# Retention, MoE layer and 8 capacity-bound experts on one core: where searches, results and stage borders are emitted

## The chip, the cores and the metric

The kernel runs on 1 core of one Trainium2 chip. The metric is the device time of one execution in microseconds, as the median of several runs; before the change it is 1059.77 us (3 runs, 1058.21 to 1059.84).

## The reference

Three layers follow one another. A retention (a linear attention with a decay per head) over 4 batches of 768 positions gives `x` of 3072 tokens by 512 features. A dense layer with 2048 hidden features follows. Then each token goes to one of 8 experts, greedily by the largest gate logit over all pairs of token and expert, with at most 384 tokens for an expert:

```python
    # retention, per step t
    state = gamma * state + einsum('bhd,bhe->bhde', k[t], v[t])
    y[t] = scale * einsum('bhd,bhde->bhe', q[t], state)
    # dense layer
    r = np.maximum(x @ w_in, 0.0)
    x = (s * (r * r) + b) @ w_out
    # experts
    logits = x @ w_gate
    for idx in np.argsort(-logits.flatten()):
        tok, e = (int(idx) // E, int(idx) % E)
        if assigned[tok] >= 0 or counts[e] >= cap:
            continue
        assigned[tok] = e
        counts[e] += 1
    for e in range(E):
        mask = assigned == e
        out[mask] = np.maximum(x[mask] @ w1[e], 0.0) @ w2[e]
```

## The kernel before

**Precision.** Every product is made of three: both operands are split into a high part (`xh`, `rh`, `gh`, `hh`, the weights' `h`) and a low part (`xl`, `rl`, `gl`, `hl`, `l`), and high·high, high·low and low·high are summed. ScalarE (ACT) makes the high part by a copy to the short format, VectorE (DVE) the low part by a subtraction, and TensorE (PE) needs both.

**Stages.** The 3072 tokens are 12 blocks of 256. Blocks 0 to 2 run through the dense layer while the weights are converted (48 to 181 us in the profiled execution), then blocks 3 to 9 (190 to 556 us). The attention of a block is made while the block ahead of it is in the dense layer; between the stages, at 181 to 190 and at 556 to 570 us, the attention of block 3 and of the last two blocks stands alone. An attention chunk is `b_part` (scores, masked by DVE to `am`, L331) and `c_part` (products with `am` and the state `sbd`, then `xh` on ACT and `xl` on DVE, L352 to L373). Blocks 10 and 11 go last: `h_pair` makes their hidden features f = 0 to 15 (for each f 12 products of 256 columns for either block, L422; Relu, Square and Copy on ACT, L425 to L434), `l_unit` their logits (L678), and `x_last` their outputs (L694), which also fill the time in which the first search runs (626 to 701 us). The experts' products follow, 701 to 1041 us: `eh_unit` (L1060, 12 products of 384 columns for each of 8 f), `eh_out` (the low part `hl`, L1069) and `ey_unit` (L1081, the outputs, from the third f on).

**A search** (generator `search`, L829 to L919) finds which expert closes next and the threshold for its tokens. It goes through six digits: `count` on PE (24 small products, L817), then on DVE `b`, `sat`, `jj`, `d`, and the next digit's `cmp` (L809). From the last count's result a chain of small DVE instructions gives `stb` and `ei`, the number of the closed expert, which SyncE reads to fetch that expert's weights `eraw`. Then `ca` (the count, written with `sat`, L891), the total `tot` (L894), `tots` on ACT (L896) and the slot product (L908, L909) follow. `begin` prepares the next search (`Lm` to `Eh` on DVE, `EH` on ACT, L765 to L809), and `index` (L927 to L961) turns slots into row numbers by `ob`, `oa`, `pay` on DVE and a product L947. `fetch` gathers the tokens `xg` by these numbers, transposes them and makes `gh` (ACT, L1001) and `gl` (DVE, L1002). `prep` splits an expert's raw weights: `h` on ACT (L1032), `l` on DVE (L1041).

**What sets the order.** Each engine executes its instructions in the order in which they were emitted. The emission is woven by hand: `Weave.unit(cost, fn)` emits one unit of PE's work and moves a clock of its own, `t`, on by `cost`; before it, each `Side` (a generator) whose due time has been reached takes a step, and what the generator yields is added to its due time. So the numbers in SY, IY, FE and BG, in ns of that clock, are pauses between the pieces of a search (SY), an index (IY), a fetch (FE) and `begin` (BG). They set no time on the chip, only what stands ahead of what.

Of the kernel before, what the change touches and what calls it, by code (L numbers as in the profile page):

```python
# [20 lines left out]
F32 = mybir.dt.float32  # L21
# [60 lines left out]
def kernel(  # L82
# [15 lines left out]
    stages=2,  # L98
    FC=((5, 0), (1, 0), (0, 1), (0, 0), (0, 0), (0, 0)),
    CY=(700, 1200),  # L100
    SY=(2900, 3200, 2700, 0, 1800, 800),
    IY=(600, 4600, 800),
    LG=(900, 880),
    FE=(9000, 3000),
    FZ=(8390, 1300),
    BG=(450,),
    WARM=24,
# [28 lines left out]
    def bank(i):  # L136
        return psum.tile([128, 512], F32, name=f"b{i}", tag=f"b{i}")
# [18 lines left out]
    work = p1.enter_context(tc.tile_pool(name="work", bufs=2))  # L156
    xpool = p1.enter_context(tc.tile_pool(name="xpool", bufs=2))
    tmp = p1.enter_context(tc.tile_pool(name="tmp", bufs=6))

    QKV = {}  # L160
    QD = {}
# [119 lines left out]
    def retention(blk, wide):  # L281

        if blk == NB - 1:

            XF.extend(tmp.tile([128, 512], F32, name="tmp").rearrange("p (a b) -> p a b", b=TB) for _ in range(2))
        elif blk == 2:
            xh = stage.tile([128, NP, TB], F32R, name="xhs", tag="sb")
            xl = stage.tile([128, NP, TB], F32R, name="xls", tag="sb")
        else:
            xh = xpool.tile([128, NP, TB], F32R, name="xh")  # L290
            xl = xpool.tile([128, NP, TB], F32R, name="xl")
        if blk < NB - 1:
            XT[blk] = (xh, xl)
        c0 = 2 * (blk % BPB)
# [19 lines left out]
        def b_part(j):  # L314

            if j == 0 and c0 == 0:
                pST[0] = bank(4)
            if wide:
                scale_next(j)
            qT, kT, kt, vt = views(j)  # L320
            ps = [bank(i) for i in ((6, 7) if not wide or j == 0 else (0, 1))]
# [58 lines left out]

        return scale_gen, b_part, c_part

    def attn(blk, wide):
        scale_gen, b_part, c_part = retention(blk, wide)
        for j in range(2):
            if not wide:
                yield from scale_gen(j)
            yield from b_part(j)
            if wide:
                yield 1500  # L390
                if j:
                    c_part(0)
                    yield 2500
            else:
                yield 4500
                c_part(j)
                yield 9000
        if wide:
            c_part(1)
            yield 2500  # L400
# [1 line left out]
    X2, R2 = {}, {}  # L402

    def split_last():
        xh = xpool.tile([128, NP, TB], F32R, name="xh")
        xl = xpool.tile([128, NP, TB], F32R, name="xl")
        XT[NB - 1] = (xh, xl)
        for i in range(2):
            ps = slice(2 * i, 2 * i + 2)
            ACT.activation(xh[:, ps], XF[i], AF.Copy)  # L410
            DVE.tensor_tensor(xl[:, ps], XF[i], xh[:, ps].bitcast(F32), op=OP.subtract)

    def h_unit(blk, f, hb):

        xh, xl = XT[blk]
        wh, wl = W[2 * f]
        ph = bank(hb)[:, 0:TB]
        n = 0
        for kc in range(KC):
            ks = slice(kc * 128, (kc + 1) * 128)  # L420
            for a, b in ((wh, xh), (wh, xl), (wl, xh)):
                PE.matmul(ph, a[:, ks], b[:, kc, :], start=(n == 0), stop=(n == 3 * KC - 1))  # L422
                n += 1
# [169 lines left out]
        convert(FC[j][1])  # L593
    conv.due = 0.0
    wv = Weave([conv])
    for u in moe1((0, 1, 2), ((4, 5), (6, 7), (0, 1)), 2):
        wv.unit(*u)
    conv_until(NF - 1)
    load_chunk(CPB)
    load_chunk(CPB + 1)  # L600
    scale_chunk(CPB)
    load_gate()
    a4 = Side(attn(3, True), wv.t)
    wv.add(a4)
    wv.until(lambda: a4.done)
    tail = Side(logits_gen())
    wv.add(tail)
    def attn2():
        for b in (NB - 2, NB - 1):
            yield from attn(b, False)  # L610

    for blk in range(3, NB - 2):
        nxt = Side(attn(blk + 1, False) if blk < NB - 3 else attn2(), wv.t + 4000 * (blk == 3))
        wv.add(nxt)
        units = moe1((blk,), ((0, 1),), 2)
        for i, u in enumerate(units):
            if i == len(units) - 2:
                while not nxt.done:
                    nxt.step()
                if blk == NB - 3:  # L620
                    split_last()
            wv.unit(*u)
    p0.close()
# [35 lines left out]
    for t in stbs:  # L659
        POOL.memset(t, 0.0)  # L660

    pair = (NB - 2, NB - 1)
    R4 = {}
    ERAW = {}

    def h_pair(f):
        rs = []
        for i, blk in enumerate(pair):
            wv.unit(1320, lambda: rs.append(h_unit(blk, f, 2 + i)))

        R4[f] = W[2 * f]
        for i, r in enumerate(rs):
            r_split(r, *(t[:, i * TB:(i + 1) * TB] for t in R4[f]))
        low_parts()

    def l_unit(f):
# [152 lines left out]
    def search(i):  # L829
# [11 lines left out]
        else:  # L841
# [3 lines left out]
            for s, w in enumerate(BW):  # L845
# [9 lines left out]
                    DVE.scalar_tensor_tensor(b, d, up, digit(key, s + 1), op0=OP.mult, op1=OP.add)  # L855
                else:
                    DVE.tensor_scalar(b, d, 1.0, None, op0=OP.add)

                sat = rt.tile([128, NT], BF, name="sat")
                sa = rt.tile([128, 1], F32, name="sa")  # L860
# [22 lines left out]
        ei = rt.tile([1, 1], I32, name="ei", bufs=3)  # L883
        DVE.tensor_scalar(ei, sm[0:1, :], -1.0, float(E), op0=OP.mult, op1=OP.add)
        EV[i] = ei
        yield SY[4]

        if not last:

            ca = rt.tile([128, 1], F32, name="ca")  # L890
            DVE.scalar_tensor_tensor(sat[:, 0:NL], iota[:, 0:NL], jj, cnt[:, 0:NL], op0=OP.is_equal, op1=OP.mult,  # L891
                                     accum_out=ca)
        tot = bank(6)
        PE.matmul(tot[:, 0:128], stb, ones_b, start=True, stop=True)  # L894
        tots = rt.tile([128, 128], BF, name="tots")
# [68 lines left out]
    def fetch(i):  # L964
# [10 lines left out]
        gh = ff.tile([128, KC, CAP], F32R, name="gh")  # L975
        gl = ff.tile([128, KC, CAP], F32R, name="gl")

        def turn(pt, t, kc):
            PE.transpose(pt[:, t * 128:(t + 1) * 128], xg[:, t, kc * 128:(kc + 1) * 128], ident)

# [13 lines left out]
        for kc in range(KC):  # L994
# [4 lines left out]
            else:  # L999
                pt = pts[kc]  # L1000
            ACT.activation(gh[:, kc, :], pt[:, 0:CAP], AF.Identity, bias=cT[:, kc:kc + 1])  # L1001
            DVE.scalar_tensor_tensor(gl[:, kc, :], pt[:, 0:CAP], cT[:, kc:kc + 1], gh[:, kc, :].bitcast(F32),  # L1002
                                     op0=OP.add, op1=OP.subtract)
            if i and kc < 3:
                prep(i, kc)
            if i and kc < KC - 1:
                yield FE[1]
        XG[i] = (gh, gl)
        HOLD.clear()

# [82 lines left out]
    def mlp(i):  # L1093
        units = []

        for f in range(NF2 + 1):
# [3 lines left out]
            for t in range(GT):  # L1100
# [2 lines left out]
                    if g >= 0:  # L1103
                        units.append((650, lambda g=g, t=t: ey_unit(i, g, t)))
                if f < NF2 and t == 0:
                    units.append((0, lambda f=f: (eh_out(i, f), prep(i, f + 3))))
                if f == NF2:
                    units.append((0, lambda t=t: e_out(i, t)))
        return units
# [128 lines left out]
```

## Time and profile before

| | |
|---|---|
| median of 3 runs | 1059.77 us |
| profiled execution, its own time | 1049.21 us |
| its span | 1047.4 us |
| PE busy | 991.0 us (95%) |
| DVE busy | 720.4 us (69%) |
| ACT busy | 459.2 us (44%) |
| GpSimd busy | 76.7 us (7%) |
| granted TensorE clock, mean | 0.99 |
| chain that ended last | PE 73%, DVE 12%, issue 8%, ACT 3%, DMA 2% |

All rows come from one profiled execution. PE's waits are listed by who released them: "PE b L894 <- DVE sat L891" means that the product of line 894 stood still until DVE's instruction of line 891 had ended. A time given for a wait is PE's idle time just before the product. An instruction's second number in a timeline is its duration, which for PE's pipelined products is longer than the distance between two starts; the distance is what counts for PE. In a table by stretches the x in brackets is the number of instructions, and PEclk the granted clock, 1.00 being 2.4 GHz.

### The profile page before, as it was taken

Reading aid. Unit: us, or ns where it says so; the run is one execution under the profiler, and the core shown is the slowest. Engines: PE = TensorE matmul, PEld = TensorE weight load, DVE = VectorE, ACT = ScalarE, POOL = GpSimd, SP = SyncE. Lnnn points to the kernel's source line nnn. Section 1 sums busy time; section 2 is a strip of 40 time slices with the busy share of each in tenths; the row PEclk is TensorE's granted clock in tenths of the full one; section 3 lists DMA queues with packets and bytes.
Section 4 is the critical chain, followed back from the end, with each engine's and each line's share of the span. In section 5 each row is a group of like instructions: output and inputs, shape, how many; then the busy total and the mean of one; then the engine's idle time right before and its main releaser. Section 6 shows DMA issues by size and latency. Waiting matters only on the chain.

```text
span 1047.4 us, 19172 instructions
## 1 busy us (share of the span) xinstructions
PE 991.0 (95%) x7548; PEld 875.5 (84%) x7548; DVE 720.4 (69%) x1794; ACT 459.2 (44%) x935; POOL 76.7 (7%) x100
## 2 busy tenths in 40 slices
PE   6899999999999999999998999889888898999997
PEld 5789988889899999899997987758766787888996
DVE  4799993687887787887744525786797877455521
ACT  1567665444344444344443661431443343434531
POOL 4100002100000000000000000011202020220211
PEclk8999999999999999999999999999999999999999
DMA  8433353431221212121120000531343424344520
GB/s 291 175 119 123 127 172 135 127 123 57 69 71 52 66 57 58 65 71 52 52 72 30 2 1 1 191 122 32 113 130 103 141 82 158 126 159 161 176 96 31
DMA packets 35035, 104.34 MB, mean 100 GB/s; under 512 B 4737, under 2 KB 5377, under 8 KB 34945
## 3 DMA queue, kind: packets, MB, share of 16 engines
q1 hardware_dynamic: 30384, 89.49, 25.9%
q0 software_dynamic: 3840, 12.59, 3.7%
q8 instruction: 59, 0.97, 0.4%
q10 hardware_dynamic: 720, 1.05, 0.3%
q14 instruction: 32, 0.25, 0.1%
HBM read 90.52 MB, written 12.58 MB: 98 GB/s over the span
## 4 chain that ended last, share of the span: by engine, by line
PE 73%; DVE 12%; issue 8%; ACT 3%; DMA 2%; POOL 1%; SPq 0%; POOLq 0%; ACTq 0%; DVEq 0%
PE b L422 24%; PE b L451 19%; PE b L1060 7%; PE b L1081 7%; PE b L694 3%; PE b L352 2%; PE b L325 2%; PE b L817 2%; PE b L362 2%; DVE l L1041 2%; ACT EH L785 1%; PE b L358 1%; DMA qdec0h<-in_dec_dram 1%; DVE raw L263 1%; POOL out_dram L1087 1%
## 5 line engine op out<-in xcount | busy, mean ns | idle before, releaser
L474 DVE SCALAR_TENSOR_TENSOR scr<-tmp,wg 128x512 bf16<-128x512 f32 x288 | 199.3, 692 | 9.0 <-ACT tmp L461 4.1
L422 PE MATMUL b<-xh,l 128*128 128x256 f32 x704 | 199.4, 283 | 3.4 <-DVE l L267 3.4
L422 PE MATMUL b<-xh,h 128*128 128x256 f32 x704 | 199.4, 283 | 1.5 <-ACT xh L372 1.5
L422 PE MATMUL b<-xl,h 128*128 128x256 f32 x704 | 199.3, 283 | 0.3 <-DVE xl L373 0.3
L425 ACT ACTIVATE r<-b 128x256 f32<-128x256 f32 x192 | 73.6, 383 | 212.2 <-PE b L422 203.4
L422 PEld LDWEIGHTS b<-xh,h 128*128 128x128 f32 x704 | 134.4, 191 | 9.6 <-ACT xh L372 1.7
L422 PEld LDWEIGHTS b<-xl,h 128*128 128x128 f32 x704 | 134.5, 191 | 6.1 <-DVE xl L373 0.5
L422 PEld LDWEIGHTS b<-xh,l 128*128 128x128 f32 x704 | 134.6, 191 | 3.8 <-DVE l L267 3.8
L451 PE MATMUL b<-h,rh 128*128 128x512 f32 x320 | 129.3, 404 | 0.0
L451 PE MATMUL b<-h,rl 128*128 128x512 f32 x320 | 125.7, 393 | 2.2 <-DVE rl L441 2.2
L451 PE MATMUL b<-l,rh 128*128 128x512 f32 x320 | 126.5, 395 | 0.0
L441 DVE TENSOR_TENSOR rl<-r,rh 128x256 fp32r<-128x256 f32 x160 | 68.5, 429 | 41.9 <-ACT rh L434 41.8
L1060 PE MATMUL b<-gh,h 128*128 128x384 f32 x256 | 90.7, 354 | 3.5 <-DVE hl L1069 3.2
L1069 DVE SCALAR_TENSOR_TENSOR hl<-b,hh 128x384 fp32r<-128x384 f32 x64 | 35.5, 554 | 79.0 <-ACT hh L1063 79.0
L1060 PE MATMUL b<-gl,h 128*128 128x384 f32 x256 | 86.6, 338 | 0.7 <-DVE gl L1002 0.7
L1060 PE MATMUL b<-gh,l 128*128 128x384 f32 x256 | 86.4, 338 | 0.0
L433 ACT ACTIVATE r<-r 128x256 f32<-128x256 f32 x192 | 79.9, 416 | 5.1
L1063 ACT ACTIVATE hh<-b 128x384 fp32r<-128x384 f32 x64 | 31.3, 489 | 115.8 <-PE b L1060 114.4
L1081 PE MATMUL b<-h,hh 128*128 128x512 f32 x192 | 78.3, 408 | 0.0
L1041 DVE TENSOR_TENSOR l<-eraw,h 128x1024 fp32r<-128x1024 f32 x64 | 77.8, 1216 | 0.7 <-ACT h L1032 0.7
L1081 PE MATMUL b<-h,hl 128*128 128x512 f32 x192 | 75.9, 395 | 0.0
L1081 PE MATMUL b<-l,hh 128*128 128x512 f32 x192 | 75.7, 394 | 0.0
(234 smaller groups left out, 1779.8 us busy)
## 6 DMA issues: line engine op xcount, KB each, us to landing
eraw<-in_w_dram SPq DMA_DIRECT2D x64, 512.0 KB, 4.0
q<-in_qkv_dram SPq DMA_DIRECT2D x36, 512.0 KB, 4.8
raw<-in_w_dram SPq DMA_DIRECT2D x32, 512.0 KB, 4.4
x2d<-tmp SPq DMA_DIRECT2D x20, 256.0 KB, 5.6
qdec<-in_dec_dram SPq DMA_DIRECT2D x18, 256.0 KB, 2.7
wg<-in_wgT_dram SPq DMA_DIRECT2D x4, 512.0 KB, 6.2
x2d<-tmp ACTq DMA_DIRECT2D x3, 256.0 KB, 3.3
first0h<-in_qkv_dram SPq DMA_DIRECT2D x2, 256.0 KB, 4.1
```

The source lines that it names most:

```text
L422: PE.matmul(ph, a[:, ks], b[:, kc, :], start=(n == 0), stop=(n == 3 * KC - 1))
L425: ACT.activation(r, ph, AF.Relu)
L433: ACT.activation(r, r, AF.Square)
L441: DVE.tensor_tensor(rl, r, rh.bitcast(F32), op=OP.subtract)
L451: PE.matmul(X2[blk][t], a[:, ts], b, start=(f == 0 and i == 0), stop=(f == NF - 1 and i == 2))
L474: DVE.scalar_tensor_tensor(scr, x, 1.0, WG[e], op0=OP.mult, op1=OP.mult, accum_out=of[:, e:e + 1])
L694: PE.matmul(XB[c][:, ns], a[:, cs], b[:, ns], start=(f == 0 and i == 0), stop=(f == NF - 1 and i == 2), skip_group_check=True)
L1041: DVE.tensor_tensor(lo, raw, hi.bitcast(F32), op=OP.subtract)
L1060: PE.matmul(PH[0], a[:, ks], b[:, kc, :], start=(kc == 0 and n == 0), stop=(kc == KC - 1 and n == 2))
L1063: ACT.activation(hh, PH[0], AF.Relu)
L1069: DVE.scalar_tensor_tensor(hl, ph, 0.0, hh.bitcast(F32), op0=OP.max, op1=OP.subtract)
L1081: PE.matmul(Y[i, t], a[:, ts], b, start=(f == 0 and j == 0), stop=(f == NF2 - 1 and j == 2))
```

## The change

Seven things are altered.

1. In `search`, `sat` with `ca` is emitted ahead of the pause SY[4], not behind it, and a new pause SY[3] stands between `b` and `sat` of each count. The pauses SY become longer.
2. In `fetch`, `gl` is emitted behind the pause (`lower`), not directly behind `gh`; FE gets shorter and has a third value.
3. In `mlp`, `eh_out` stands behind the third output unit of an f, not the first.
4. In the first border, the last units of block 2 are emitted between the parts of block 3's attention, which uses banks 2 and 3 for the first chunk's scores.
5. In block 9, the pauses in the last two blocks' attention are (2800, 2500) instead of (4500, 9000), and `low_parts` is emitted ahead of `split_last`.
6. `x` of even and odd blocks lies side by side in one tile, so `h_pair` makes one product of 512 columns for blocks 10 and 11, and one Relu, Square and Copy.
7. In blocks 0 to 2, the second and third block swap their banks.

```diff
-    SY=(2900, 3200, 2700, 0, 1800, 800),
+    SY=(4300, 3500, 2900, 450, 2600, 1200),
     IY=(600, 4600, 800),
-    FE=(9000, 3000),
+    FE=(6500, 2800, 600),
...
-    for u in moe1((0, 1, 2), ((4, 5), (6, 7), (0, 1)), 2):
+    units = moe1((0, 1, 2), ((4, 5), (0, 1), (6, 7)), 2)
+    for u in units[:-2]:
         wv.unit(*u)
...
-    a4 = Side(attn(3, True), wv.t)
-    wv.add(a4)
-    wv.until(lambda: a4.done)
+    _, b_part, c_part = retention(3, True)
+    for _ in b_part(0):
+        pass
+    wv.unit(*units[-2])
+    c_part(0)
+    for _ in b_part(1):
+        pass
+    x_unit(2, NF - 1, None, (0,))
+    c_part(1)
+    x_unit(2, NF - 1, None, (1,))
+    x_out(2)
...
-            yield from attn(b, False)
+            yield from attn(b, False, (2800, 2500))
...
                 if blk == NB - 3:
+                    low_parts()
                     split_last()
...
     def h_pair(f):
-        rs = []
-        for i, blk in enumerate(pair):
-            wv.unit(1320, lambda: rs.append(h_unit(blk, f, 2 + i)))
+        ph = bank(2 + f % 2)
+        for i in range(2):
+            wv.unit(1300, lambda: h_part(f, ph, XP, range(2 * i, 2 * i + 2)))
+        r = r2[:, f % 2]
+        ACT.activation(r, ph, AF.Relu)
         R4[f] = W[2 * f]
-        for i, r in enumerate(rs):
-            r_split(r, *(t[:, i * TB:(i + 1) * TB] for t in R4[f]))
+        r_split(r, *R4[f])
         low_parts()
...
                     DVE.tensor_scalar(b, d, 1.0, None, op0=OP.add)
+                yield SY[3]
                 sat = rt.tile([128, NT], BF, name="sat")
...
         EV[i] = ei
-        yield SY[4]
         if not last:
             ca = rt.tile([128, 1], F32, name="ca")
             DVE.scalar_tensor_tensor(sat[:, 0:NL], iota[:, 0:NL], jj, cnt[:, 0:NL], op0=OP.is_equal, op1=OP.mult,
                                      accum_out=ca)
+        yield SY[4]
+
         tot = bank(6)
...
             ACT.activation(gh[:, kc, :], pt[:, 0:CAP], AF.Identity, bias=cT[:, kc:kc + 1])
-            DVE.scalar_tensor_tensor(gl[:, kc, :], pt[:, 0:CAP], cT[:, kc:kc + 1], gh[:, kc, :].bitcast(F32),
-                                     op0=OP.add, op1=OP.subtract)
-            if i and kc < 3:
+            low.append((kc, pt))
+            if not i:
+                lower()
+            elif kc < 3:
                 prep(i, kc)
-            if i and kc < KC - 1:
-                yield FE[1]
+            if i:
+                yield FE[1] if kc < KC - 1 else FE[2]
+                lower()
...
                 if f < NF2 and t == 0:
-                    units.append((0, lambda f=f: (eh_out(i, f), prep(i, f + 3))))
+                    units.append((0, lambda f=f: prep(i, f + 3)))
+                if f < NF2 and t == GT - 1:
+                    units.append((0, lambda f=f: eh_out(i, f)))
```

Three places show what moves. On ACT, at the end of search 0, before (`h` is the high part of the first expert's raw weights, `EH` and `tmp` belong to the next search and to the last outputs):

```order
L785 ACTIVATE EH<-Eh 128x768 x4
L896 ACTIVATE tots<-b_7407 128x128
L1032 ACTIVATE h_7419<-eraw 128x1024
L785 ACTIVATE EH<-Eh 128x768
L698 ACTIVATE tmp<-b_6989,sb 128x512
```

and after:

```order
L799 ACTIVATE EH<-Eh 128x768 x4
L712 ACTIVATE tmp<-b_6666,sb 128x512
L714 DMA x2d<-tmp 128x512
L1057 ACTIVATE h_7114<-eraw 128x1024
L911 ACTIVATE tots<-b_7119 128x128
L712 ACTIVATE tmp<-b_6670,sb 128x512
```

`tots` stood ahead of the first split and now stands behind it. On DVE, at the end of search 6, before (`sat,ca` is the count that the total waits for):

```order
L884 TENSOR_SCALAR ei<-sm 1x1
L1069 SCALAR_TENSOR_TENSOR hl<-b_10604,hh 128x384
L1041 TENSOR_TENSOR l_10592<-eraw,h_10591 128x1024
L891 SCALAR_TENSOR_TENSOR sat,ca<-c_6327,jj,b_10614 128x33
L900 TENSOR_SCALAR s_10686<-c_6327,sm 128x1
```

and after:

```order
L897 SCALAR_TENSOR_TENSOR stb_6324<-mx,sm,eq 128x24
L899 TENSOR_SCALAR ei<-sm 1x1
L904 SCALAR_TENSOR_TENSOR sat,ca<-c_6307,jj,b_10774 128x33
L1094 SCALAR_TENSOR_TENSOR hl<-b_10758,hh 128x384
L915 TENSOR_SCALAR s_10850<-c_6307,sm 128x1
```

The count moved ahead of the expert's work. On PE, at the slot products of search 4, before (products with `hh` or `hl` are outputs of the running expert, those with `gh` or `gl` the hidden features of the next one):

```order
L908 MATMUL b_9604<-stb_6344,strict 128x48
L909 LDWEIGHTS tots
L909 MATMUL b_9604<-strict,tots 128x48
L1081 MATMUL b_9053<-h_9125,hh 128x512
L1081 MATMUL b_9053<-l_9126,hh 128x512
L1081 MATMUL b_9053<-h_9125,hl 128x512
L1081 MATMUL b_9053<-h_9223,hh 128x512
L1081 MATMUL b_9053<-l_9224,hh 128x512
L1081 MATMUL b_9053<-h_9223,hl 128x512
L1060 MATMUL b_9661<-gh,h_9142 128x384
```

and after:

```order
L1106 MATMUL b_9081<-l_9256,hh 128x512
L1106 MATMUL b_9081<-h_9255,hl 128x512
L923 LDWEIGHTS strict
L923 MATMUL b_9597<-stb_6324,strict 128x48
L924 LDWEIGHTS tots
L924 MATMUL b_9597<-strict,tots 128x48
L1085 MATMUL b_9614<-gh,h_9283 128x384
L1085 MATMUL b_9614<-gl,h_9283 128x384
L1085 MATMUL b_9614<-gh,l_9284 128x384
```

The slot products stood six outputs ahead of the next expert's first product and now stand directly ahead of it.

## Rows read from the trace of the kernel before

**Rows 1.** Waits of PE: us in total, times, longest.

```profile
PE b L894 <- DVE sat L891: 11.8, 7, 3.2
PE b L817 <- DVE cmp L809: 6.1, 5, 2.1
...
PE b L817 <- ACT EH L785: 4.6, 6, 1.4
...
PE b L1060 <- DVE hl L1069: 3.2, 1, 3.2
...
PE b L422 <- ACT xh L372: 1.5, 1, 1.5
...
PE b L894 <- DVE ei L884: 1.8, 1, 1.8
PE b L817 <- DVE dg L798: 1.1, 1, 1.1
```

**Rows 2.** Stretches: length, busy time of PE, PEld, DVE, ACT, GpSimd, PEclk, DMA.

```profile
667.00:670.40 3.40, 3.40 (x35) 2.87 (x36) 3.23 (x10) 1.07 (x2) 0.00 (x0) 0.50 0.80 265
810.40:813.80 3.40, 3.20 (x29) 2.90 (x30) 2.56 (x8) 1.82 (x3) 0.00 (x0) 0.50 0.07 25
871.80:875.30 3.50, 3.25 (x13) 2.63 (x13) 2.46 (x10) 1.80 (x3) 0.00 (x0) 0.51 0.45 150
...
885.00:1040.00 155.00, 155.00 (x854) 138.54 (x853) 67.50 (x100) 60.49 (x93) 23.65 (x36) 1.00 0.39 128
...
701.00:885.00 184.00, 160.18 (x1494) 138.21 (x1494) 142.53 (x485) 68.18 (x110) 21.84 (x30) 0.98 0.33 105
556.00:570.00 14.00, 10.74 (x110) 8.43 (x109) 5.73 (x13) 3.47 (x10) 1.56 (x5) 1.00 0.06 18
...
190.00:556.00 366.00, 365.68 (x2754) 330.64 (x2755) 284.46 (x760) 160.81 (x389) 2.40 (x3) 1.00 0.22 68
```

**Rows 3.** Chain that ended last: start, length, products, one f and first outputs.

```profile
593.43 2.87 PE b L422 x24
...
623.38 1.85 PE b L694 x8
```

**Rows 4.** Timeline of DVE: start, duration, in searches 0 and 6.

```profile
653.54 0.26 DVE L861 SCALAR_TENSOR_TENSOR sat<-b,rem,ones_b 128x33 bf16<-128x33 f32 x1 [1.82 <-PE b L817]
...
655.98 0.13 DVE L884 TENSOR_SCALAR ei<-sm 1x1 int32<-1x1 f32 x1
...
664.67 1.22 DVE L1041 TENSOR_TENSOR l<-eraw,h 128x1024 fp32r<-128x1024 f32 x1
...
870.10 0.13 DVE L884 TENSOR_SCALAR ei<-sm 1x1 int32<-1x1 f32 x1
...
871.76 0.23 DVE L891 SCALAR_TENSOR_TENSOR sat<-c,jj,b 128x33 bf16<-128x33 f32 x1
```

**Rows 5.** Timeline of PE: slot of search 0.

```profile
657.14 0.20 PE L908 MATMUL b<-stb,strict 128*128 128x48 bf16 x1
```

**Rows 6.** Timeline of PE: search 4, slot, two h products, wait.

```profile
801.49 0.20 PE L908 MATMUL b<-stb,strict 128*128 128x48 bf16 x1
...
803.02 0.34 PE L1060 MATMUL b<-gh,h 128*128 128x384 f32 x1
...
805.13 0.33 PE L1060 MATMUL b<-gh,h 128*128 128x384 f32 x1
...
810.60 0.69 PE L1060 MATMUL b<-gh,h 128*128 128x384 f32 x1 [3.23 <-DVE hl L1069]
```

**Rows 7.** Timeline of ACT: search 0, total and first split.

```profile
656.59 0.28 ACT L896 ACTIVATE tots<-b 128x128 bf16<-128x128 f32 x1 [21.61 <-PE b L894]
660.89 1.06 ACT L1032 ACTIVATE h<-eraw 128x1024 fp32r<-128x1024 f32 x1 [4.03 <-DMA eraw<-in_w_dram]
```

**Rows 8.** Timeline of ACT: search 4, the expert's first high part.

```profile
809.47 0.48 ACT L1063 ACTIVATE hh<-b 128x384 fp32r<-128x384 f32 x1
```

More of the change, by code (lines that the diff above doesn't have):

```diff
@@ L158 @@
     tmp = p1.enter_context(tc.tile_pool(name="tmp", bufs=6))
+    XP = [xpool.tile([128, 2, NP, TB], F32R, name="x" + p, bufs=1) for p in "hl"]
     QKV = {}
@@ L289, in retention @@
         else:
-            xh = xpool.tile([128, NP, TB], F32R, name="xh")
-            xl = xpool.tile([128, NP, TB], F32R, name="xl")
+            xh, xl = (t[:, blk % 2] for t in XP)
         if blk < NB - 1:
@@ L320, in b_part @@
             qT, kT, kt, vt = views(j)
-            ps = [bank(i) for i in ((6, 7) if not wide or j == 0 else (0, 1))]
+            ps = [bank(i) for i in ((6, 7) if not wide else (0, 1) if j else (2, 3) if blk == 3 else (6, 7))]
             for p in range(NP):
@@ L381, in retention, with attn @@
         return scale_gen, b_part, c_part
-    def attn(blk, wide):
+    def attn(blk, wide, gaps=(4500, 9000)):
         scale_gen, b_part, c_part = retention(blk, wide)
@@ L394, in attn @@
             else:
-                yield 4500
+                yield gaps[0]
                 c_part(j)
-                yield 9000
+                yield gaps[1]
         if wide:
@@ L404, in split_last @@
     def split_last():
-        xh = xpool.tile([128, NP, TB], F32R, name="xh")
-        xl = xpool.tile([128, NP, TB], F32R, name="xl")
+        xh, xl = (t[:, (NB - 1) % 2] for t in XP)
         XT[NB - 1] = (xh, xl)
@@ L411, in split_last, with h_part @@
             DVE.tensor_tensor(xl[:, ps], XF[i], xh[:, ps].bitcast(F32), op=OP.subtract)
+    def h_part(f, ph, x, kcs):
+        xh, xl = x
+        wh, wl = W[2 * f]
+        for kc in kcs:
+            ks = slice(kc * 128, (kc + 1) * 128)
+            for n, (a, b) in enumerate(((wh, xh), (wh, xl), (wl, xh))):
+                PE.matmul(ph, a[:, ks], b[..., kc, :], start=(kc == 0 and n == 0), stop=(kc == KC - 1 and n == 2))
     def h_unit(blk, f, hb):
-        xh, xl = XT[blk]
-        wh, wl = W[2 * f]
         ph = bank(hb)[:, 0:TB]
[L418 to L423, printed above, removed]
+        h_part(f, ph, XT[blk], range(KC))
         r = work.tile([128, TB], F32, name="r", bufs=2)
@@ L660 @@
         POOL.memset(t, 0.0)
-    pair = (NB - 2, NB - 1)
     R4 = {}
+    r2 = rt.tile([128, 2, 2 * TB], F32, name="r2", tag="EH")
     ERAW = {}
     def h_pair(f):
-        rs = []
-        for i, blk in enumerate(pair):
-            wv.unit(1320, lambda: rs.append(h_unit(blk, f, 2 + i)))
+        ph = bank(2 + f % 2)
[3 more added lines that the diff above has]
+        ACT.activation(r, ph, AF.Relu)
         R4[f] = W[2 * f]
-        for i, r in enumerate(rs):
-            r_split(r, *(t[:, i * TB:(i + 1) * TB] for t in R4[f]))
+        r_split(r, *R4[f])
         low_parts()
@@ L976, in fetch, with lower @@
         gl = ff.tile([128, KC, CAP], F32R, name="gl")
+        low = []
+        def lower():
+            while low:
+                kc, pt = low.pop(0)
+                DVE.scalar_tensor_tensor(gl[:, kc, :], pt[:, 0:CAP], cT[:, kc:kc + 1], gh[:, kc, :].bitcast(F32),
+                                         op0=OP.add, op1=OP.subtract)
         def turn(pt, t, kc):
```

## Prediction

> **What bounds the kernel now.** I read the page first: TensorE (PE) is busy for 991.0 of 1047.4 us and no other engine for more than 720.4, so the end is set by PE's work plus the time in which PE stands still. A change that leaves PE's products alone can only move the standing time. Next comes the table of PE's waits [rows 1], then PE's busy time by stretch [rows 2]. Between 190 and 556 us PE has no idle time worth speaking of, nor from 885 us to the end; it stands still at the two stage borders (14.00 - 10.74 = 3.3 us at the second [rows 2]) and above all between 626 and 885 us, where the experts' searches run under the last output products and experts 0 to 3. The waits there are on a search's own chain: the total of a search behind `sat` (11.8 us in 7 waits) and `ei` (1.8), counts behind `cmp`, `EH` and `dg` (6.1 + 4.6 + 1.1), one expert product behind `hl` (3.2) [rows 1]. Together that is 28.6 us. On top come three stretches of 3.4 us in which the granted clock is 0.50 [rows 2], that is 1.2 instead of 2.4 GHz, each behind a standstill; one costs about half its length, 1.7 us.
>
> The change adds no arithmetic of weight. So the question is which of these waits go, and which ones the new order makes.
>
> **Step 1, totals.** Before, `sat` with `ca` (L891) is emitted after the pause SY[4], so whatever DVE got in between stands ahead of it: in search 6 `ei` starts at 870.10, and `sat` at 871.76 behind an `hl` and an `l` [rows 4], and PE's total waits for it. After, it stands directly behind `ei`, and PE has 3.5 to 4.4 us of its own products between the last count and the total (for instance 15 output products of 0.231 us [rows 3]). The chain from the last count's result to `ei` is 655.98 - 653.54 = 2.4 us, plus `ei` itself [rows 4]. The cover is longer than the chain, so 11.8 + 1.8 go: **-13.6 us**. Bound: where an `l` stands in the chain some 2 us stay in two of the seven, so -9 to -13.6.
>
> **Step 2, counts.** The pauses between counts grow (SY[1] 3200 to 3500, and SY[3] adds 450), so PE's work from count to count rises from about 3.6 to about 4.5 us, and with it the cover of `cmp`, `EH` and `dg`: 6.1 + 4.6 + 1.1 = **-11.8 us**. What stays of these waits is in step 6(d).
>
> **Step 3, second border.** The last two blocks' attention is spread over block 9 (pauses 2800 and 2500 for 4500 and 9000), so its four parts no longer stand in a row at 556 to 570, and `low_parts` goes ahead of `split_last`, so the 1.3 us wait on `rl` has its operand earlier. Block 9's other products hide them. The row of that stretch gives **-3.3 us** [rows 2]; if DVE, which then carries two blocks' attention beside the gate, falls behind, up to 2 us come back as waits on `rl`.
>
> **Step 4, one h product.** Per f, 24 products of 256 columns take 2.87 us in the chain; 8 products of 512 columns take 1.85, so 12 take 2.78 [rows 3]. 16 x 0.09 = **-1.4 us**. ACT does one Relu, Square and Copy of 512 columns instead of two of 256, under the 3.2 us that the next f takes. The Trainium skill (TensorE: Matmul & The Clock Gate, Back-to-back issue gap) gives the isolated gap as N / 2.4 + 2.5 ns, which for these two forms is 109 and 216 ns; by that, as an estimate, the step would bring 16 x (24 x 0.1092 - 12 x 0.2158) = 0.5 us. The rows show 0.120 and 0.231 us instead, and they decide.
>
> **Step 5, first border.** Block 3's two attention chunks are laid between the last products of block 2. But chunk 1's masks stand behind chunk 0's `xl` on DVE, and `c_part(1)` needs them; and the last `x` product now stands between `c_part(1)` and block 3. Before, this border costs PE the waits on `xh` of 1.5 [rows 1] and smaller ones. I put one such wait more against what the laying apart saves: **+0.6 us**, between -1 and +1.5 (the `xh` wait once more). The swap of banks in blocks 0 to 2 changes no product and no wait that the table lists: 0.
>
> **Step 6, new waits.** These are read from the order of the changed program against durations of the old one.
> (a) Search 0: before, `tots` (656.59) stands ahead of the first weight split `h`, which waits 4.03 us for its DMA and starts at 660.89 [rows 7]. After, ACT does that split first, then `tots`, and PE's second slot product needs `tots`. From `ei` to the split's start it is 660.89 - 655.98 = 4.9 us, the split takes 1.06, `tots` 0.28 [rows 4, 7]: 6.2 us behind `ei`, some 8.7 behind the last count, where PE has 4.4 us of other work before slot. **+4.4 us** (bounds 2 and 5, as the weight's transfer lands sooner or later).
> (b) Searches 0 to 5: from slot's start to the last `pay` DVE needs 664.67 - 657.14 = 7.5 us [rows 4, 5]. Before, the index product stands behind the next search's first count; after, it stands ahead of it, with 6.1 to 6.3 us of products between slot and index (in search 4: 36 expert products of 2.11 / 12 us [rows 6]). 7.5 + 0.1 - 6.3 = 1.3 us each, more where an `l` is queued in between; in two of the six the wait in (c) covers it. **+6.5 us** (0 to 8).
> (c) Expert starts: a search now lasts as long as an expert, so the burst slot, `begin`, `index` (7.5 us on DVE) falls on the start of the next expert in searches 2 to 5. There the first two `hl` have only the 2.1 us of one product each as cover, since no output products are due yet. In search 4 slot stands directly ahead of the expert's first product; the third needs `hl` of the first, 2 x 2.11 = 4.2 us after slot, while `hl` is done at 7.5 + 0.6: 3.9 us. The trace has one such case: slot at 801.49, then six output products and two h products, and PE on again at 810.60 after 3.23 us [rows 6], and ACT's `hh` at 809.47 just ahead of it [rows 8]. In search 3 it is the second `hl`, behind burst and an `l`: 7.5 + 1.2 + 0.6 - 5.8 = 3.5; searches 2 and 5 give 1.6 and 1.0. Sum 10.0. And `eh_out` moves behind the third output, so that an expert's last `hl` has 1.2 us of products for cover instead of 2.6; where the last count's chain of 2.4 us is ahead of it, PE waits: 4.5 us over searches 2, 3, 4 and 6. **+14.5 us** (5, if only the case of [rows 6] recurs with half as much again, to 17).
> (d) Counts behind a `cmp` that stands behind an `l`, total of search 5, and a few gathers, FE[0] being 6500 for 9000: seven waits of 0.4 to 1.4. **+5 us** (2 to 7).
> Three stretches at half clock remain three, for waits as long as those that preceded them: 0, with 1.7 us for each more or fewer.
>
> **Sum.** Removed: 13.6 + 11.8 + 3.2 (the old `hl` wait) + 3.3 + 1.4 = 33.3. Added: 0.6 + 4.4 + 6.5 + 14.5 + 5 = 31.0. Net -2.3 us, so the profiled execution of 1049.21 would become 1046.9. That execution is 10.6 us under the median of the runs, 1059.77; I take this distance as unchanged and predict **1057.5 us**.
>
> **Rivals.**
> *The new waits are mostly not there.* DVE carries 142.5 of 184 us between 701 and 885 [rows 2]; a search drawn out by a quarter leaves it more room, and if a queue that I take as full is empty when a burst begins, half of (a) to (d) vanishes. For it: the covers of steps 1 and 2 are the same mechanism at work. Against it: each burst is one unbroken piece of 7.5 us whatever the load. 15 us of new waits instead of 30.4 give 1057.5 - 15.4 = **1042**.
> *Slower, by the bursts at the expert starts.* The long waits of (a) and (c), some six of over 2 us, each throw PE to half clock as the standstill ahead of 810.40 did, and step 1 brings its low end. Three more stretches cost 5.1, step 1 brings 4.6 less: 1057.5 + 9.7 = **1067**. It decides as soon as what is added exceeds the 33.3 us removed by more than 2.1, that is from 4.4 us above my tally of 31.0. For it: three stretches at 0.50 exist [rows 2]. Against it: as many waits over 2 us before were followed by none. The Trainium skill (TensorE: Matmul & The Clock Gate, HAM oscillation: how this bites in real kernels) says that an idle TensorE falls back to half rate and pays for it again at each gap; by it this rival would be the rule, while the trace shows it after some waits only.
> *The change does not do what it says.* PE's products are the same but for step 4. If the total still waits as it did and the rest evens out, the time stays at **1060**.
>
> **How the numbers follow.** 0.2%, 2.1 us, is about what a measurement of this kernel can tell from no change: faster means under 1057.6, slower over 1061.9. My sum has a chance of 0.5, with its own range 1052 to 1063, of which 0.26 lies below 1057.6, 0.18 within the band and 0.06 above it; the first rival has 0.2, the second 0.25, no effect 0.05. Faster: 0.26 + 0.2 = 0.46. Same: 0.18 + 0.05 = 0.23. Slower: 0.06 + 0.25 = 0.31. The range that leaves out the outer half of each rival is 1042 to 1067.
>
> **What would show it.** Step 1: no wait of `tot` on `sat` in PE's table. Step 3: no gap at the end of block 9. Step 4: 2.78 us per f in the chain. (a): `tots` of search 0 some 6 us behind `ei`, and PE's slot waiting for it. (b): a wait of the index product on `pay` in most searches. (c): the largest entry of PE's wait table is `hl`, at the starts of experts 2 to 5. The forecast is wrong on the fast side if PE's wait table between 626 us and the last search sums to under 25 us, on the slow side if it is over 40.

## The result, and the profile after

The changed kernel takes 1044.58 us (median of 4 runs, 1038.84 to 1046.19) against 1059.16 us of the kernel before in the same series: a ratio of 0.986 with a 95% interval of 0.984 to 0.989, 14.6 us less. The forecast was 1057.5 us, 2 us less.

The profiled execution of after has a span of 1041.5 us where before had 1047.4: 5.9 us, not 14.6. That of after (1043.38 us by its own time) is one of the four timed runs; that of before (1049.21) is none of its four, 1058.21 to 1059.84. Most of what follows is about these two numbers: which waits went and came, and why the medians lie farther apart than the two traces.

PE's waits of the kernel after, from the table of waits (who waited, for whom: us in total, times, longest); these rows answer to [rows 1]:

```profile
PE b L1085 <- DVE hl L1094: 8.4, 3, 3.5
PE b L962 <- DVE pay L956: 4.9, 4, 1.6
...
PE b L1002 <- DMA big<-x2d,idx: 4.8, 8, 1.4
PE b L923 <- ACT tots L911: 4.1, 1, 4.1
PE b L1106 <- DVE hl L1094: 4.0, 4, 2.0
...
PE b L909 <- DVE sat L904: 1.4, 1, 1.4
...
PE b L831 <- DVE cmp L823: 0.9, 2, 0.5
...
PE b L831 <- ACT EH L799: 0.4, 1, 0.4
```

The old list is nearly empty: of 11.8 us on `sat`, 1.4 are left, of 6.1 on `cmp` 0.9, of 4.6 on `EH` 0.4. In its place stands a new one, of `hl`, `pay`, the gather and `tots`. Summed over the rows of the searches and experts, PE waits 29.5 us after and 32.1 before. There the change gained 2.6 us of waits and no more.

By stretch (length, busy time of PE, PEld, DVE, ACT, GpSimd, PEclk, DMA share and GB/s), the kernel after; the first row answers to the row of 556 to 570 us in [rows 2], the other three are its stretches at half clock between 600 and 1000 us:

```profile
555.00:572.00 17.00, 17.00 (x106) 14.37 (x105) 5.96 (x17) 7.27 (x15) 1.31 (x5) 1.00 0.14 46
...
660.60:664.00 3.40, 2.90 (x9) 2.32 (x9) 2.42 (x10) 1.22 (x4) 0.00 (x0) 0.50 0.75 298
797.10:800.50 3.40, 3.40 (x34) 2.96 (x33) 1.39 (x4) 0.81 (x2) 0.00 (x0) 0.51 0.74 214
831.30:834.70 3.40, 3.40 (x10) 2.40 (x9) 0.00 (x0) 1.05 (x3) 1.42 (x3) 0.50 0.23 82
```

PE no longer stands still at the second border. And of the chain that ended last (start, length, products), two pieces of the hidden features of blocks 10 and 11, for [rows 3]:

```profile
579.70 2.75 PE b L419 x12
582.45 0.47 PE b L692 x2
```

One f takes 2.75 + 0.47 = 3.22 us; before it took 2.87 [rows 3] and the same pair behind it, 3.33 between two starts.

### The profile page after: what moved, and what is told of

It is laid out like the page before. It is cut to its first block, busy times and chain, and to the rows that moved or that the text cites. A ratio compares the mean times of both kernels' runs of the same rounds, so it can differ in the third digit from the quotient of the medians.

```text
span 1041.5 us, 18741 instructions
## 1 busy us (share of the span) xinstructions
PE 989.6 (95%) x7356; PEld 861.5 (83%) x7356; DVE 714.3 (69%) x1778; ACT 452.8 (43%) x887; POOL 77.7 (7%) x100
## 4 chain that ended last, share of the span: by engine, by line
PE 68%; DVE 15%; issue 7%; DMA 5%; ACT 3%; POOL 2%; SPq 0%; POOLq 0%; DVEq 0%; ACTq 0%
PE b L419 22%; PE b L452 17%; PE b L1106 7%; PE b L1085 7%; DMA big<-x2d,idx 3%; PE b L708 2%; PE b L353 2%; PE b L326 2%; PE b L363 2%; PE b L831 2%; DVE raw L265 1%; POOL big L985 1%; DVE l L1066 1%; DVE raw L253 1%; DVE rl L442 1%
## 5 line engine op out<-in xcount | busy, mean ns | idle before, releaser
L419 PE MATMUL b<-xh,l 128*128 128x256 f32 (+1 forms) x640 | 188.3, 294 | 3.4 <-DVE l L269 3.4
L419 PE MATMUL b<-xh,h 128*128 128x256 f32 (+1 forms) x640 | 188.8, 295 | 0.8 <-ACT xh L373 0.8
L419 PE MATMUL b<-xl,h 128*128 128x256 f32 (+1 forms) x640 | 188.1, 294 | 0.3 <-DVE xl L374 0.3
L426 ACT ACTIVATE r<-b 128x256 f32<-128x256 f32 x160 | 61.2, 383 | 192.6 <-PE b L419 184.3
L419 PEld LDWEIGHTS b<-xh,h 128*128 128x128 f32 x640 | 122.1, 191 | 11.0 <-ACT xh L373 1.3
L419 PEld LDWEIGHTS b<-xl,h 128*128 128x128 f32 x640 | 122.0, 191 | 7.9 <-DVE xl L374 0.5
L419 PEld LDWEIGHTS b<-xh,l 128*128 128x128 f32 x640 | 122.1, 191 | 6.5 <-DVE l L269 3.8
L434 ACT ACTIVATE r<-r 128x256 f32<-128x256 f32 (+1 forms) x176 | 77.0, 438 | 5.6
L452 PEld LDWEIGHTS b<-h,rl 128*128 128x128 f32 x320 | 60.4, 189 | 15.2 <-DVE rl L442 1.5
```

The costliest lines, as they stand in the source:

```text
L419: PE.matmul(ph, a[:, ks], b[..., kc, :], start=(kc == 0 and n == 0), stop=(kc == KC - 1 and n == 2))
L434: ACT.activation(r, r, AF.Square)
L452: PE.matmul(X2[blk][t], a[:, ts], b, start=(f == 0 and i == 0), stop=(f == NF - 1 and i == 2))
```

## The experiments

Every ratio below is against the kernel before, run in the same series (a set of runs taken together) on the same chip. The medians of before, unchanged, differ from series to series: 1052.49 and 1051.41 us in two series on chip 0, 1057.76 and 1051.15 in two on chip 10, and 1059.16 in the series of the result. After itself was run only in the two series in which before took longest (1059.16 and 1057.76). So a ratio also carries what before did in its series; differences are taken within a series, and between series the spans and waits of the traces stand beside the ratios.

### The kernel before, traced again

No edit. Two further series of the kernel before.

> The kernel before, unchanged. Its profiled execution was 1049.2 us and the median of its runs 1059.2; after's are 1043.4 and 1044.6. Theory A: the executions of before spread, and the profiled one was a short one by chance; then this profile comes out some us longer, its extra time stands as longer waits between 626 and 885 us, and the runs spread over several us. Theory B: before's profiled executions are always about 10 us shorter than its timed ones; then the profile is again 1047 to 1050 and the runs 1058 to 1060. The ratio to before is 1.000 in both.

> The kernel before once more, for a second trace of an execution that is longer than the 1047.4 us of the first. Theory: the waits of PE behind 626 us are those of the first two traces to 0.2 us, and what differs is the time at half clock (24 us in the first, 34 in the second). Rival: some transfer or wait at the start differs by several us.

Measured: 0.9995 [0.998, 1.0009] and 1.0004 [0.9991, 1.0016]. The profiled executions have spans of 1051.7 and 1052.1 us, 4.3 and 4.7 more than the first. PE's waits of the first of the two new traces:

```profile
PE b L894 <- DVE sat L891: 11.8, 7, 3.2
PE b L817 <- DVE cmp L809: 6.1, 5, 2.1
...
PE b L817 <- ACT EH L785: 4.8, 6, 1.4
...
PE b L1060 <- DVE hl L1069: 3.2, 1, 3.2
```

They are [rows 1] again, to 0.2 us; over the searches and experts they sum to 32.4, and to 32.5 in the other trace, after 32.1 in the first. What differs is the clock. The same execution by stretch:

```profile
635.00:638.40 3.40, 3.40 (x9) 2.65 (x9) 1.81 (x8) 0.00 (x0) 0.00 (x0) 0.50 0.02 5
669.10:672.50 3.40, 3.40 (x12) 2.33 (x8) 2.66 (x5) 0.60 (x2) 0.00 (x0) 0.50 0.64 214
812.50:815.90 3.40, 3.40 (x32) 3.18 (x31) 3.03 (x10) 1.11 (x2) 0.00 (x0) 0.50 0.16 22
839.80:846.60 6.80, 5.93 (x20) 5.21 (x20) 4.69 (x18) 1.35 (x3) 0.00 (x0) 0.50 0.25 77
877.30:880.70 3.40, 3.40 (x13) 3.36 (x13) 2.23 (x5) 1.05 (x2) 0.00 (x0) 0.50 0.54 159
```

Five stretches, one of double length, 20.4 us, where the first trace had three [rows 2], 10.3 us. The landmarks of the program (the totals of the eight searches) run apart at these places and hardly elsewhere: counted from the first product of block 0, by 1.6 us up to the first total, and by 2.7 us more in the stretch at 839.8. The third trace has 17 us of such stretches there, at 669.4, 812.7, 840.0 (of double length) and 877.6 us, and one more at the first border, behind a wait of 1.5 us:

```profile
191.50:194.90 3.40, 3.40 (x18) 3.40 (x17) 2.46 (x6) 1.35 (x4) 0.91 (x1) 0.50 0.95 281
```

So theory A holds in its first half: the executions spread (1049.26 to 1055.49 us in one series), and the profiled one was a short one. Its second half fails: the kernel before waits the same each time, and the extra time is not in longer waits but in how many of its standstills are followed by a stretch at half clock. Neither theory has what the medians show: 1051.02 us here, where the series of the result had 1059.16. Theory B expected 1058 to 1060 again. These 8 us between series are the larger part of the 10.6 us, and what makes them is open. The rival of the second expectation, a wait at the start, falls: the start differs by under 1 us.

### The searches' part alone

```diff
-    SY=(2900, 3200, 2700, 0, 1800, 800),
+    SY=(4300, 3500, 2900, 450, 2600, 1200),
...
+                yield SY[3]
...
-        yield SY[4]
         if not last:
...
+        yield SY[4]
```

> Before with the searches' part of the change alone: sat with ca ahead of the pause, and the new pauses SY; eh_out, gl, FE, borders and h product as before. My sum: waits of the total on sat (11.8) and most of cmp, EH and dg (11.8) go; the new waits (a) 4.1 on tots, (b) some 5 on pay and those of hl at expert starts (8) come: about 5 us less than before, 1054, if the median moves as the profile; if the executions of before carry some 9 us more of the waits that this removes than its profile shows (rival), 1046 to 1048.

Measured: 0.9874 [0.9856, 0.9893], 14.6 us less than before. By the ratio that is as much as the whole change; by the span of its trace, 1035.9 us for 1041.5 and 1041.1 in the two of after, it is 5 us better. My sum had said 5, so it was too low here. The rival's figure, 11 to 13 us less, is nearer, but not for its reason: no trace of before has more than 32.5 us of waits. PE's waits of this kernel:

```profile
PE b L948 <- DVE pay L942: 5.5, 4, 2.0
...
PE b L1061 <- DVE hl L1070: 4.8, 4, 3.4
PE b L909 <- ACT tots L897: 4.3, 1, 4.3
...
PE b L1061 <- DVE gl L1003: 2.3, 1, 2.3
...
PE b L895 <- DVE sat L890: 1.2, 3, 0.8
...
PE b L980 <- DMA big<-x2d,idx: 0.3, 1, 0.3
```

Over the searches and experts 20.5 us, 11.6 fewer than before. Against after, the gather has 0.3 in place of 4.8, the output products' waits on `hl` are missing, and those at the experts' starts are 4.8 for 8.4. So these belong to other edits of the change, not to the longer searches; two of these edits are undone one by one below.

### The total alone

```diff
-        yield SY[4]
         if not last:
...
+        yield SY[4]
```

> Before with only sat and ca moved ahead of the pause SY[4]; all pauses as before. It tells step 1 from step 2. My sum: of 13.6 us of waits of the total, those go in which work stands between ei and sat; but SY[4] 1800 leaves PE the same 2.7 to 2.9 us of products between last count and total, against a chain of 2.4 to 2.8, so most go: 8 to 11 us less than before, and the counts' waits (11.8) stay. Rival: the gain of the searches' part lies in the longer pauses; then this is within 3 us of before.

Measured: 0.9953 [0.9937, 0.9969], 5 us less. PE's waits:

```profile
PE b L817 <- DVE cmp L809: 6.5, 6, 2.1
PE b L894 <- DVE sat L889: 6.0, 7, 1.6
PE b L817 <- ACT EH L785: 5.2, 7, 1.4
```

The seven waits on `sat` shrink from 11.8 to 6.0 and don't go: with the old pauses PE reaches the total before the chain has ended, `hl` or no `hl`. The order alone takes 5.8 of the 13.6 us of step 1 (the 1.8 us on `ei` stay, too); the rest of it and all of step 2 come from the pauses. Both expectations missed, mine on the high side.

### Borders and the one h product alone

The kernel after with the searches, the fetches and `eh_out` as before (the edit is the experts' part of the diff, undone).

> Before with the rearranged borders and the one h product alone; searches, fetches and eh_out as before. My sum: 3.3 at the second border and 1.4 to 1.7 at the h products go, the first border costs about what it did: 4 to 5 us less, 1055. The rival, by which the whole gain lies in the searches: within 1.5 us of before.

Measured: 0.994 [0.9923, 0.9958], 6.3 us less, a little more than the sum; the rival falls. The waits over searches and experts are 31.9, as before.

### The first search's `tots`

```diff
-                if n >= 2 * NF and n % 4 == 0 and (0, f) in ERAW:
+                if n >= 2 * NF and n % 4 == 0 and (0, f) in ERAW and TOTD:
...
         ACT.activation(tots, tot[:, 0:128], AF.Copy)
+        TOTD.append(i)
...
-    FILLED, SPLIT0 = [], []
+    FILLED, SPLIT0, TOTD = [], [], []
```

> After, with the weight splits of expert 0 held back until the first search's tots has been emitted, so that tots stands ahead of the first split on ACT as in before. Theory: PE's wait of 4.1 us at the slot product of search 0 goes, and with it the stretch at half clock that follows it at 660.6 us (up to 1.7 us): 4 to 6 us less than after, about 1039 to 1040. Rival: the splits come later, the first expert's weights are late, and the wait moves to the first expert's products: no gain.

What it removes is seen best in after itself. On ACT (start, duration, what it waited for), and PE's slot product behind it:

```profile
659.82 1.06 ACT L1057 ACTIVATE h<-eraw 128x1024 fp32r<-128x1024 f32 x1 [7.89 <-DMA eraw<-in_w_dram]
660.79 0.26 ACT L911 ACTIVATE tots<-b 128x128 bf16<-128x128 f32 x1
...
661.10 0.20 PE L923 MATMUL b<-stb,strict 128*128 128x48 bf16 x1 [4.15 <-ACT tots L911]
```

`tots` needs only PE's total, but stands behind a copy that waits for its DMA. With the edit, on ACT:

```profile
653.15 0.28 ACT L911 ACTIVATE tots<-b 128x128 bf16<-128x128 f32 x1 [3.60 <-PE b L909]
...
657.66 1.06 ACT L1058 ACTIVATE h<-eraw 128x1024 fp32r<-128x1024 f32 x1 [1.54 <-DMA eraw<-in_w_dram]
```

Measured: 0.984 [0.9821, 0.986]. The wait of 4.1 us is gone and nothing takes its place: from the first logits' product to the first transpose of gathered tokens it is 108.8 us where after has 113.8, so a little more than the wait. The stretch at half clock behind the wait is gone with it, as expected, but later ones came: 17.1 us of them between 600 and 1000 us, where the two traces of after have 10.2 and 13.7. As a ratio this is 0.002 to 0.004 under after (0.9862 and 0.9881 in its two series), with intervals that overlap, and the two were run in different series. So that the wait goes is shown, and what it is worth in the median is not, by this run alone.

### After again, and three edits undone

After once more, beside its variants on one chip:

> After, unchanged, so that the variants stand beside it on one chip. Theory: its waits are those of the trace of after to 0.2 us each, and its executions differ only by how many stretches of 3.4 us at half clock follow the same waits (three to six), as in the two profiles of before. Ratio to before 0.986 again, spread of the runs 3 to 8 us.

Measured: 0.9881 [0.985, 0.9911], runs of 1042.84 to 1046.05. Its waits are those of the first trace (`hl` 8.5, `pay` 5.0, `tots` 4.1, `hl` at the experts' ends 4.0) but for the gather, 2.9 for 4.8. Four stretches of 3.4 us at half clock.

`eh_out` behind the first output unit, as before:

```diff
                 if f < NF2 and t == 0:
-                    units.append((0, lambda f=f: prep(i, f + 3)))
-                if f < NF2 and t == GT - 1:
-                    units.append((0, lambda f=f: eh_out(i, f)))
+                    units.append((0, lambda f=f: (eh_out(i, f), prep(i, f + 3))))
```

> After with eh_out behind the first output unit again, as in before. Theory: the four waits of output products on hl at experts' ends (4.0 us in the trace of after) go, 3 to 5 us less than after, since the last low part of an expert is emitted two output units earlier on DVE. Rival: hl then stands ahead of the counts' results on DVE and waits for hh there, so that counts and totals wait for cmp and sat instead: within 1.5 us of after.

Measured: 0.9826 [0.9794, 0.9857], 4.1 us less than after. The four waits of output products on `hl` are gone, and 2.3 of the 8.5 us at the experts' starts too. The gather's wait is longer (4.6 for 2.9), and the sum falls from 27.8 to 24.3. As expected.

The fetch's first pause as before:

```diff
-    FE=(6500, 2800, 600),
+    FE=(9000, 2800, 600),
```

> After with FE[0] 9000 instead of 6500: the gathered tokens are transposed 2.5 us of emission later. Theory: the eight waits for the gather (4.8 us) go nearly all, as in the run with the searches' part alone, which has 0.3 us of them: 3 to 5 us less than after. Rival: the transposes and gh then bunch at an expert's end, and hl, gl or the first h products wait for them: no gain.

Measured: 0.9816 [0.9786, 0.9846], 6.6 us less than after, more than expected. No wait for the gather is left in PE's table, and the sum over searches and experts falls from 27.8 to 22.2. Of PE's waits that are left:

```profile
PE b L1106 <- DVE hl L1094: 5.7, 2, 4.6
PE b L1085 <- DVE hl L1094: 5.5, 4, 3.8
...
PE b L1085 <- DVE gl L998: 1.8, 1, 1.8
```

The gather's 2.9 us are half of the 5.6 that went: `hl` at the experts' starts has 5.5 for 8.5, and the counts and the total wait less. The rival is there in part: `hl` at the experts' ends takes 5.7 for 4.0, and `gl` 1.8.

All three together:

> After with all three: tots of search 0 ahead of the first weight split, eh_out behind the first output unit, FE[0] 9000. If the three waits (4.1 on tots, 4.0 on hl at experts' ends, 4.8 on the gather) are independent, 10 to 13 us less than after and two stretches at half clock fewer, 1028 to 1031 where before is 1052; if they hide one another, no better than the run with tots alone, 1035.

Measured: 0.9735 [0.9702, 0.9768], 14.2 us less than after in the same series (1029.79 for 1043.94). PE's waits:

```profile
PE b L963 <- DVE pay L957: 7.3, 5, 2.0
PE b L1086 <- DVE hl L1095: 4.9, 4, 3.4
...
PE b L1086 <- DVE gl L999: 1.8, 1, 1.8
...
PE b L1003 <- DMA big<-x2d,idx: 1.0, 2, 0.5
```

16.7 us over searches and experts, for 27.8. In time the three edits add up: two of them alone gave 4.1 and 6.6 us in this series, and all three 14.2, which leaves 3.5 for `tots`, within its 2 to 4. In the waits they do not act row by row: the sum fell by 11.1 us, close to the 11.0 of the three waits that they aim at, but 1.0 of the gather stays, `hl` at the experts' starts fell by 3.6, and `pay` rose by 2.3 and `gl` by 1.8. The two stretches fewer at half clock that were expected did not come: the trace has 20.5 us of them, where the trace of after in this series has 13.7.

### Late `gl`

The version above, and `gl` directly behind `gh` again with FE (9000, 3000):

```diff
-    FE=(9000, 2800, 600),
+    FE=(9000, 3000),
...
-            low.append((kc, pt))
+            DVE.scalar_tensor_tensor(gl[:, kc, :], pt[:, 0:CAP], cT[:, kc:kc + 1], gh[:, kc, :].bitcast(F32),
+                                     op0=OP.add, op1=OP.subtract)
```

> The version with tots, eh_out and FE[0] undone, and gl emitted directly behind gh again with FE (9000, 3000): of the experts' part, only the totals and the pauses SY are left of the change. From the first gather to the last product the searches' part alone took 336.7 us, that version 341. Theory: late gl is what costs these 4 us, so 0.970 of before and 3 to 5 us less than that version. Rival: waits sum to the same 17 us in both and the 4 us are the stretches at half clock (20 us there, 7 in the searches' part alone behind the first gather), which fall as they fall: within 2 us of that version, 0.972 to 0.975.

Measured: 1028.28 us, 0.9777 [0.975, 0.9803]; before was 1051.15 in this series and 1057.76 in the other. By the medians it is 1.5 us less than the version above, by the ratios 0.004 more; the waits sum to 17.0 and 16.7. The theory's 3 to 5 us are not there. The rival has the waits right and the ratio wrong (it said 0.972 to 0.975). As the two were run in different series, a difference of some us either way is not excluded. What this version keeps of the change is the searches' part, the borders and the one h product, and with `tots` put back it adds up: 14.6, 6.3 and 2 to 4 us by their own ratios are 23 to 25, and it takes 22.9 us off a before of 1051.15, as theirs were of 1052.49. Its trace has two stretches of 3.4 us at half clock between 600 and 1000 us and a span of 1024.4, the one above has 20.5 us of them and 1029.9: again equal waits and another clock.

### Room for the index

The version with all three, and

```diff
-    IY=(600, 4600, 800),
+    IY=(600, 6400, 800),
-    BG=(450,),
+    BG=(900,),
```

> The version with tots, eh_out and FE[0] undone, and with IY[1] 6400 instead of 4600 and BG 900 instead of 450: PE then has 8.4 us of products between slot and index where pay needs 7.6. Theory (b): the five waits of the index product on pay (7.3 us in that version's trace) go; the gather is asked for some 2 us later, and FE[0] 9000 covers it; hl stands inside the burst instead of behind it, so its waits shrink too: 6 to 9 us less than that version, 0.967 of before. Rival: pay was late only because DVE is full, so another wait (gather, cmp or hl) takes its place: within 2 us of that version, 0.9735 of before.

Measured: 0.9871 [0.9851, 0.9891], worse than that version; both expectations missed. By the ratios it is worse by 14 us, by the medians by 7, by the spans by 5 (1034.6 for 1029.9); it was run on another chip, so the size is open. PE's waits:

```profile
PE b L1086 <- DVE gl L999: 4.9, 4, 1.7
...
PE b L1086 <- DVE hl L1095: 3.0, 4, 1.3
PE b L708 <- ACT tmp L712: 3.0, 1, 3.0
PE b L831 <- DVE cmp L823: 2.9, 2, 1.7
...
PE b L1086 <- DVE l L1067: 2.1, 4, 0.5
```

The 7.3 us on `pay` are gone and `hl` is smaller, as theory (b) has it, but `gl`, `cmp`, `l` and `tmp` now hold PE up, and over searches and experts the waits are 20.5 us, for 16.7. So the rival's reason, that another wait takes the place, is what the trace shows. The two pauses were changed at once, so it is open which of them brings which.

## Why the prediction was right or wrong

The direction held, and the time lies in the stated range, 13 us under the forecast. That the range held is luck. The time is outside the sum's own range, 1052 to 1063; it is inside the stated one by its low end of 1042 alone, and that came from the first rival, by which half of (a) to (d) would not be there. 26.9 of their 30.4 us were. The sign of being wrong did not show either: PE's waits sum to 29.5 us, between 25 and 40, since the error lay elsewhere. Term by term, in us, from the traces:

| step | predicted | measured |
|---|---|---|
| 1, totals | -13.6 | -13.6, and 1.4 comes back in search 3 under (d) |
| 2, counts | -11.8 | -11.8, and 1.3 comes back under (d) |
| old wait on `hl` | -3.2 | -3.2 |
| 3, second border | -3.3 | -4.6 (block 3 to first logits' product: 382.0 for 386.6) |
| 4, one h product | -1.4 | -1.7 (3.21 us per f for 3.32) |
| 5, first border | +0.6 | +0.8 (block 0 to block 3: 151.7 for 150.9) |
| 6a, `tots` | +4.4 | +4.1 |
| 6b, index on `pay` | +6.5 | +4.9, 4 waits |
| 6c, `hl` at starts and ends | +14.5 | +12.4 (8.4 and 4.0) |
| 6d, the rest | +5 | +5.5 (1.4 `sat`, 1.3 counts, 2.8 more on the gather) |
| sum | -2.3 | -7.2 |

The waits on `gl` and `gh` of before (0.9 us) went too and stand in no step. The first trace of before and that of after both have 10.2 us at half clock between 600 and 1000 us, and their spans differ by 5.9 us, so some 1 to 2 us of the table are not found in the span.

The mechanisms were right, and each stood where it was named. (a) was in the order of ACT to be read. So was (c): in search 3 of after, DVE's slot result, the last of the burst and the `hl` behind it, and PE's third product behind that:

```profile
787.76 0.20 DVE L926 SCALAR_TENSOR_TENSOR s<-b,stb 128x48 f32<-128x48 f32 x1
...
794.47 0.55 DVE L956 TENSOR_TENSOR pay<-oa,c 128x384 f16<-128x384 f16 x1
794.94 1.22 DVE L1066 TENSOR_TENSOR l<-eraw,h 128x1024 fp32r<-128x1024 f32 x1
796.07 0.55 DVE L1094 SCALAR_TENSOR_TENSOR hl<-b,hh 128x384 fp32r<-128x384 f32 x1
...
796.68 0.44 PE L1085 MATMUL b<-gh,h 128*128 128x384 f32 x1 [3.52 <-DVE hl L1094]
```

Predicted 3.5 for search 3 and 3.9 for search 4, measured 3.52 and 3.54. The mis-sized terms are (b) and (c), by 2 us each on the high side, and step 3, which was taken from the idle time of one stretch where 1.3 us more went around it. The second rival's mechanism is there, but not its count: in the trace of after the waits of 4.15, 3.52 and 2.02 us are followed by half clock and that of 3.54 us is not; the old stretches went with their waits, so there are three as before.

What failed is the step from the trace to the median: "That execution is 10.6 us under the median of the runs, 1059.77; I take this distance as unchanged". The distance is 1.2 us in after (1043.38 profiled, 1044.58 median). Part of before's distance is the clock of the traced execution: two further traces have the same waits and 1053.4 and 1053.9 us, with 20.5 us at half clock behind 100 us each, where the first has 10.2. The other part lies between series: the same kernel has medians of 1051.0 to 1052.5 us in three later ones, and 1059.16 and 1057.76 in the two in which after was run. No trace of before was taken in the runs of these two, so what they add is not known. "Three remain three" is true of the first two traces only: before has six in each of its other traces (one of double length counted as two), after three and four.

Against the two longer traces of before, after is 10 to 11 us shorter in span. Of that, 3.4 to 5.1 us are half of the difference in time at half clock, and the rest, 5 to 8 us, is about what the table gives. The medians are 14.6 and 13.8 us apart. With the clock's part counted in, 3 to 4 us of that are open, without it 6 to 9. Whether it may be counted in is not shown: in the series with after beside before on one chip the mean clocks of the runs were the same (0.983). Before loses about 0.8 us for each 0.001 of the clock there (1052.5 at 0.988, 1061.7 at 0.977), after about 0.5 (1042.8 at 0.987, 1046.1 at 0.980), each worked out from two runs, so that at 0.987 they are 10.5 us apart (1053.35 and 1042.84). What after gains on a before of 1051 us was not measured.

The second thing learned is that the change was two. Its searches' part alone takes 14.6 us off and its borders with the one h product 6.3, together 20.9. The moved `eh_out` and FE[0] at 6500 cost 4.1 and 6.6 us in the series of after. By these four the whole would be worth 10.2 us, near the difference of the spans to the longer traces, and less than its searches' part alone. Undoing the two and the place of `tots` brings 0.9735. The prediction had priced them as parts of (c) and (d), and as costs, but had not said that they buy nothing.

## What to carry to other kernels

An in-order engine between a slow load and a short chain is worth a look at its order first: here a copy that waited for its DMA stood ahead of the copy that the tensor engine waited for, and a condition of one word removed a wait of 4.1 us. When a burst of small instructions is spread to the period of the loop beside it, it falls on the same place in every turn; look for that place, and see whether it is the one where the loop has least cover. (That another place is better is not shown here: the one run that gave the index more room had other waits instead.) And before a sum is set against one trace, trace the unchanged kernel a second time, in the series in which the change is timed: equal waits with another time show how much of the distance is the clock.

## What the runs showed of the hardware

Three traces of one program agree in every wait behind 626 us to 0.3 us, and two of them have spans 4.3 and 4.7 us longer than the first. They have 20.5 us in stretches of 3.4 us (or twice that) in which the granted clock is 0.50, where the first has 10.2; half of the difference is 5.1 us. These stretches begin behind a standstill of PE, of 1.1 to 3.2 us, and the same standstill is followed by one in some executions and not in others: the wait of 3.19 us for the total of search 5 at 840 us in two traces of three. A long standstill is not needed: in the version with room for the index a stretch of 6.8 us begins at 845.5 us, and just ahead of it PE had waits of 0.58 and 0.51 us. The time at half clock did not fall with the waits: 20.5 us of it in the version with 16.7 us of waits, 6.8 in another with 17.0.
